# The recurrence's slot table: stages five slots apart, the new state formed ahead of the outputs, the solver, merges and compactions at other slots

## The chip, the cores and the metric

The kernel runs on one core of one Trainium2 chip. The metric is the time of one execution in microseconds (us) on the device. The core's engines work side by side, each through its own list of instructions in the order of the program: PE (TensorE, matrix products into PSUM), DVE (VectorE), ACT (ScalarE), POOL (GpSimd) and SP (SyncE, which here issues nearly all DMAs). An instruction that has to wait holds everything behind it on its engine.

## The reference, cut to what matters

For each of 32 pairs of batch and head a 40 by 40 state is carried through 768 steps, and each step gives an output row. The rows are then the tokens of two MLP layers in fp32.

```
for t in range(S):                      # S = 768, D = 40, B*H = 32
    y[:, :, t] = einsum('bhd,bhde->bhe', rt, state)
    Sa = einsum('bhde,bhe->bhd', state, at)
    state = state * wt[:, :, None, :] - einsum('bhd,bhe->bhde', Sa, bt) + einsum('bhd,bhe->bhde', vt, kt)
x = y.transpose(0, 2, 1, 3).reshape(3072, 320)
h = x @ w_in;  r = maximum(h, 0);  x = (r * r) @ w_out          # 320 -> 2048 -> 320
h = x @ w_in2; x = (h * cos(h)) @ w_out2
```

## The kernel before

**Chunks and periods.** The 768 steps are cut into 12 chunks of 64. `Program.period(c)` writes out the work around chunk `c`: 42 slots, and in each slot a few calls. `at(t, f)` puts a call into slot `t`; the calls of a slot run in the order in which `at` was called. There is no scheduler: the order in which the Python code calls the engines is the order on each engine, and semaphores are all that holds one engine against another. A slot has no time of its own.

**What a period does.** For chunk `c` there are four groups `g`, each a generator `state(c, g)` with six steps: `pq` (what the carried state gives), `px`, `pu`, `py` (each a set of small matmuls into PSUM and a copy or masked multiply out of it), and `pm`, which transposes the new state `MT` into `M0d` for the next chunk. Groups 0 and 1 run in the first half of a period, 2 and 3 in the second. Before the change `py` is followed, in one step, by four DVE operations a group: `MT += `, `sz += ` (outputs), `MT *= lam`, `yt = sz * lam` (outputs).

**The solver.** A chunk needs the inverse of a triangular matrix, for all 32 pairs. Its 32 by 32 diagonal blocks are inverted by `solve`, a chain of 31 pairs of instructions (`ttmp`, line 448, and `T`, line 451), each waiting for the one before, and a last copy (line 454). In period `c` it runs for chunk `c + 1`: on DVE in period 0 (as a chain fed in after other DVE instructions), on POOL from period 1 on, `rate[t]` instructions in slot `t`. `gt` and `gt_out` make and store the matrix (`Ls<-ga`, line 421; its last quarter is made in slots 0 to 2 of period `c` and stored in slot 3), `solve_load` (slot 6) loads it (`T<-kti`, `L<-Ls`, `l21<-Ls`), `solve_store` stores the result (`Tn<-L`, `Ts<-T`, lines 461 and 463), and `load_t` loads it in another layout (`t<-Tn`, `tt<-Ts`, lines 470 and 476). `merge` (matmuls `pw` and `pt`, copies of ACT at lines 491 and 504) makes the full inverse from it at the start of the next period.

**Other work in the slots.** `load_kb` (line 338, `cin<-cin`, 832 KB) loads k and b of chunk `c + 2`, `compact_kb` scales them on DVE (four instructions `cin<-cin` of 104 x 512), `compact_a` scales a (`at<-at`), `decay` makes `lam`. `mov_load` and `rv_load` bring v and r; `y_store` stores outputs (`xs<-yt`, line 547), and `load_x` (slot 2 of each second period) loads them as tokens (`xf<-xs`).

**The MLP in between.** From period 2 on, each slot also takes on average 64.2 / 42 = 1.53 pairs of matmuls of layer 0 (`h`, line 839, and `po`, line 795). A hidden tile goes through ACT (`g`, `gh`, lines 693 to 695) and POOL (`gl`, line 696). `h` has one PSUM buffer here, so PE cannot start a hidden tile before ACT has read the last one.

**The weights' pieces.** The MLP's weights come as 64-bit words that are taken apart on the chip, in every slot one step of `Weights`. For the second layer (`second`) a piece starts every five slots: its load (`w<-moe`, line 183, SP) in slot 5k of its own count, then in slot 5k + 4 `clamp` (ACT `u<-w`, line 167, and a DVE instruction), in 5k + 5 `bits` (DVE), in 5k + 6 `add` (POOL `u<-u,w`, line 179), and in 5k + 10 the store (`w2f<-u`, line 278, SP). The tiles `w` and `u` have two buffers each, so the clamp of a piece waits for its own load and for the store of the piece before the last, and these two stand side by side on SP. Counted in slots of the period, the pairs of load and store of the periods 4 to 10 stand at the slots that leave the rest 1, 4, 2, 0, 3, 1, 4 when divided by five. Before that, in period 2 and the start of period 3, `rest` has a piece every four slots, and `first` has one of 704 KB every five until about slot 30 of period 1.

The functions that the change touches, with the line numbers of the profile:

Of the kernel before, what the change touches and what calls it, by code (L numbers as in the profile page):

```python
# [15 lines left out]
ALU = mybir.AluOpType  # L16
# [265 lines left out]
class Attn:  # L282
# [269 lines left out]
    def state(self, c, g):  # L552
# [42 lines left out]
        last = c == self.nch - 1  # L595
        if not last:
            self.vec.tensor_tensor(mt[0:104], yv[0:104, :, 64:104], mt[0:104], op=ALU.add)
        if c:
            self.vec.tensor_tensor(sz[0:104], yv[0:104, :, 0:64], sz[0:104], op=ALU.add)
        if not last:  # L600
            self.vec.tensor_tensor(mt[0:104], mt[0:104],
                                   self.lam[(c + 1) % 3][:, 4 * g:4 * g + 4, 64:65].to_broadcast([104, 4, 40]), op=ALU.mult)
# [271 lines left out]

ALONE = 2
FIRST, RATE = 9, 64.2 / 42


class Program:
# [131 lines left out]
    def period(self, c):  # L1013
# [6 lines left out]
        def at(t, f, *args):  # L1020
            todo.setdefault(t, []).append((f, args))

        for half in range(2):
            for k in range(5):
                for q in range(2):
                    at(20 * half + 4 * k, step, st[2 * half + q])
        for h, t0 in enumerate((5, 5) if c == 0 else (2, 2) if more else (4, 12)):
            mg = A.merge(h)
            at(t0, step, mg)
            at(t0 + (4 if c and more else 2), step, mg)  # L1030
        at(2, A.rv_load, c, 2)
        at(6, A.rv_load, c, 3)
        at(6, A.mov_load, c, 2)
        at(8, A.pmat, c, 2)
        at(14, A.mov_load, c, 3)
        at(16, A.pmat, c, 3)
        at(17, A.y_store, c, 0)
        at(37, A.y_store, c, 1)
        if more:
            for t in (0, 1, 2):  # L1040
                at(t, step, self.gts[c + 1])
            at(2, A.gt_in, c + 1, 0, 0)
            at(4, A.gt_in, c + 1, 0, 1)
            at(3, A.gt_out, c + 1, 1, 0)
            at(3, A.gt_out, c + 1, 1, 1)
            at(8, A.gt_in, c + 1, 1, 0)
            at(10, A.gt_in, c + 1, 1, 1)
            at(6, A.solve_load, c + 1)
            for t in range(9, 36):
                rate[t] = 3 if t % 3 == 0 else 2  # L1050
            rate[36] = 100
            at(37, A.solve_store)
            at(38, A.load_t)
            at(23, A.rv_load, c + 1, 0)
            at(25, A.rv_load, c + 1, 1)
            at(26, A.mov_load, c + 1, 0)
            at(28, A.pmat, c + 1, 0)
            at(34, A.mov_load, c + 1, 1)
            at(38, A.pmat, c + 1, 1)
        if c + 2 < nch:  # L1060
            for t in (0, 2, 3, 4, 5, 6, 7, 9):
# [7 lines left out]
            at(28, A.compact_a, c + 2, 1)  # L1069
            self.gts.setdefault(c + 2, A.gt(c + 2))  # L1070
            for t in (24, 25, 26, 32, 33, 34, 36, 37, 38):
                at(t, step, self.gts[c + 2])
            at(37, A.gt_out, c + 2, 0, 0)
            at(39, A.gt_out, c + 2, 0, 1)
        if c + 3 < nch:
            self.dcs[c + 3] = A.decay(c + 3)
            at(30, A.load_w, c + 3)
            for t in (34, 35, 36, 38, 40, 41):
                at(t, step, self.dcs[c + 3])
        for t in range(42):  # L1080
            if more and t == 9:
# [116 lines left out]
```

## Time and profile before

| | |
|---|---|
| time, median of 3 runs | 1291.59 us (1290.32 to 1296.13) |
| the profiled execution | 1293.38 us, of which 1291.6 us are its span |
| PE busy | 1075.1 us, 83% |
| DVE, ACT, POOL busy | 712.9, 702.4, 671.1 us (55%, 54%, 52%) |
| granted TensorE clock, mean | 0.897 of full speed |
| chain that ended last, by engine | PE 50%, POOL 16%, DMA 12%, DVE 10%, SP's queue 5% |

How to read it: the span is cut by the program into a start without the MLP (to about 200 us), the periods with the MLP in between (to about 864 us), and the rest of the MLP alone (864 to 1291.6 us). In the last part PE is busy nearly all the time; in the periods it is not. The shares of the whole span say little: what a change in the periods is worth is read in a period.

### The profile page before, as it was taken

The page shows a single profiled execution, that of the slowest core. Times are in us where ns is not written, and L with a number is a line of the kernel's source. Part 1 is how long each engine was busy: PE and PEld are TensorE (multiplying, and loading weights), DVE is VectorE, ACT ScalarE, POOL GpSimd, SP SyncE. Part 2 cuts the span into 40 slices and gives each one's busy share as a digit, 9 for nine tenths or more (in the row PEclk, how much of TensorE's full clock was granted, in tenths as well). Part 3 has the DMA queues.
Part 4 walks back from the last instruction along what each step waited for, and adds up shares of the span by engine and source line. Part 5 has one row for each costly group of instructions (what it writes and reads, how often), then busy time and mean ns, then how long its engine had stood idle before and what let it go on. Part 6 is the DMA issues. An engine that isn't in the chain of part 4 may idle for free.

```text
span 1291.6 us, 27044 instructions
## 1 busy us (share of the span) xinstructions
PE 1075.1 (83%) x10242; PEld 902.2 (70%) x10242; DVE 712.9 (55%) x1450; ACT 702.4 (54%) x1492; POOL 671.1 (52%) x1067
## 2 busy tenths in 40 slices
PE   3245636787879898969797899799999999999997
PEld 3144536666657676757676678578889999999996
DVE  6869765576656665736665546221197343444432
ACT  4133644566566566655656556556556565655554
POOL 4112585685739482838474747423586333333332
PEclk9985555788979898988898889899999999999998
DMA  6473744546373838373745454413031010101000
GB/s 178 83 170 92 174 113 97 115 94 137 71 182 93 171 82 190 93 156 84 159 128 119 113 131 114 88 41 134 19 117 41 5 46 1 46 1 45 1 21 24
DMA packets 281168, 121.74 MB, mean 94 GB/s; under 512 B 231013, under 2 KB 259173, under 8 KB 279885
## 3 DMA queue, kind: packets, MB, share of 16 engines
q1 hardware_dynamic: 279195, 119.24, 38.8%
q8 instruction: 83, 1.36, 0.4%
q10 hardware_dynamic: 1834, 0.69, 0.2%
q14 instruction: 56, 0.46, 0.1%
HBM read 91.31 MB, written 28.57 MB: 93 GB/s over the span
## 4 chain that ended last, share of the span: by engine, by line
PE 50%; POOL 16%; DMA 12%; DVE 10%; SPq 5%; issue 4%; ACT 3%; POOLq 0%; ACTq 0%; DVEq 0%
PE h L839 22%; PE pt L785 13%; PE po L795 7%; DMA cin<-cin 6%; POOL T L451 5%; POOL ttmp L448 4%; POOL gl L696 3%; DMA w2f<-u 2%; POOL u L179 2%; PE px L573 2%; DVE u L142 2%; DVE T L451 1%; DVE ttmp L448 1%; DVE cin L142 1%; PE pu L581 1%
## 5 line engine op out<-in xcount | busy, mean ns | idle before, releaser
L839 PE MATMUL h<-xh,ws 128*128 128x512 f32 x960 | 333.8, 411 | 22.5 <-ACT g L693 22.2
L839 PE MATMUL h<-xl,ws 128*128 128x512 f32 x576 | 235.5, 409 | 0.0
L839 PEld LDWEIGHTS h<-xh,ws 128*128 128x128 f32 x960 | 185.9, 195 | 66.2 <-ACT g L693 26.2
L724 POOL TENSOR_TENSOR gl<-g,gh 128x512 fp32r<-128x512 f32 x96 | 125.2, 1304 | 190.9 <-ACT gh L723 163.6
L179 POOL TENSOR_TENSOR u<-u,w 128x256 int32<-128x256 int32 (+2 forms) x104 | 75.4, 725 | 222.0 <-DVE u L142 142.3
L696 POOL TENSOR_TENSOR gl<-g,gh 128x512 fp32r<-128x512 f32 x96 | 126.7, 1320 | 116.8 <-ACT gh L695 108.9
L142 DVE TENSOR_SCALAR u<-u 128x256 f32<-128x256 f32 (+2 forms) x208 | 72.5, 349 | 172.9 <-ACT u L167 171.2
L795 PE MATMUL po<-gh,ws 128*128 128x512 f32 x480 | 142.8, 422 | 0.3 <-DVE o L142 0.3
L448 POOL TENSOR_TENSOR ttmp<-T,L 128x126 f32<-128x126 f32 (+22 forms) x310 | 124.9, 403 | 34.0 <-DMA L<-Ls 14.0
L451 POOL TENSOR_TENSOR T<-T,ttmp 128x126 f32<-128x126 f32 (+22 forms) x310 | 131.3, 424 | 19.3
L785 PE MATMUL pt<-ws,gh 128*128 128x320 f32 x768 | 128.1, 308 | 0.5 <-DVE g L142 0.4
L839 PEld LDWEIGHTS h<-xl,ws 128*128 128x128 f32 x576 | 112.5, 195 | 20.2
L785 PEld LDWEIGHTS pt<-ws,gh 128*128 128x128 f32 x768 | 119.9, 188 | 8.3 <-DVE g L142 0.6
L142 DVE SCALAR_TENSOR_TENSOR g<-n,h 128x512 f32<-128x512 int32 x96 | 66.0, 687 | 103.3 <-ACT n L704 100.4
L704 ACT ACTIVATE n<-h 128x512 int32<-128x512 f32 x96 | 57.3, 596 | 119.9 <-PE h L839 119.8
L693 ACT ACTIVATE g<-h 128x512 f32<-128x512 f32 x96 | 57.0, 594 | 109.8 <-PE h L839 109.2
L407 PE MATMUL pgt<-at,cin 40*128 40x104 f32 x768 | 72.1, 329 | 52.1 <-DVE at L142 21.4
L795 PEld LDWEIGHTS po<-gh,ws 128*128 128x128 f32 x480 | 94.0, 201 | 24.0 <-issue 1.7
L142 DVE TENSOR_TENSOR g<-g,h 128x512 f32<-128x512 f32 x96 | 65.8, 685 | 71.7 <-ACT g L708 71.7
L167 ACT ACTIVATE u<-w 128x256 f32<-128x256 f32 (+2 forms) x104 | 40.8, 392 | 117.9 <-DMA w2f<-u 73.7
L407 PEld LDWEIGHTS pgt<-at,cin 40*128 40x128 f32 x768 | 62.0, 230 | 59.1 <-issue 24.9
L795 PE MATMUL po<-gl,ws 128*128 128x512 f32 x288 | 85.5, 400 | 0.0
(100 smaller groups left out, 2308.5 us busy)
## 6 DMA issues: line engine op xcount, KB each, us to landing
rv<-rv SPq DMA_DIRECT2D x48, 256.0 KB
cin<-cin SPq DMA_DIRECT2D x11, 832.0 KB
w<-moe SPq DMA_DIRECT2D x12, 704.0 KB
w<-moe SPq DMA_DIRECT2D x40, 160.0 KB
Ls<-ga SPq DMA_DIRECT2D x48, 128.0 KB
L<-Ls SPq DMA_DIRECT2D x48, 128.0 KB
wr<-w2f SPq DMA_DIRECT2D x16, 352.0 KB
w<-moe SPq DMA_DIRECT2D x20, 256.0 KB
```

Of the source, the lines that this page charges most:

```text
L142: fn(*args, **kwargs)
L179: self.nc.gpsimd.tensor_tensor(t.bitcast(I32), u.bitcast(I32), w[:, :, 0], op=ALU.add)
L407: nc.tensor.matmul(pv[par][:, j], self.kb[r0:r0 + 40, p0 + j].rearrange("p h b -> p (h b)"), self.at[r0:r0 + 40, p0 + j], start=True, stop ...
L448: eng.tensor_tensor(tv, T[:, 0:r, j:j + 1].to_broadcast([128, r, n]), L[:, j:j + 1, j + 1:32].to_broadcast([128, r, n]), op=ALU.mult)
L451: eng.tensor_tensor(T[:, 0:r, j + 1:32], T[:, 0:r, j + 1:32], tv, op=ALU.add)
L693: nc.scalar.activation(g, h, AF.Relu)
L696: self.later.append((2, lambda: nc.gpsimd.tensor_tensor(gl, g, gh, op=ALU.subtract)))
L704: nc.scalar.activation(n, h, AF.Copy, bias=0.25, scale=float(np.float32(1.0 / (2.0 * np.pi))))
L724: nc.gpsimd.tensor_tensor(gl, g, gh, op=ALU.subtract)
L785: nc.tensor.matmul(self.pos[j][:, 0:DM], x[:, 128 * j:128 * j + 128], wo[:, DM * ws:DM * ws + DM], start=(f == 0 and x is gh and ws == 0), ...
L795: nc.tensor.matmul(self.pos[m], wo[:, 128 * ws:128 * ws + 128], x, start=(f == 0 and k in (0, 2, 4)), stop=(f == NF - 1 and k in (5, 6, 7)))
L839: nc.tensor.matmul(h, wi[:, ws], x[:, kt], start=(k == 0), stop=(k == 7))
```

## The change

The diff changes numbers in the slot table and the order inside one step, and no instruction's form. In `state`, `MT *= lam` moves up behind `MT +=`, and a `yield` is put in: the two output operations become a step of their own, one (first half: slot 16) or two (second half: slot 37) slots later. The first five stages stand five slots apart instead of four, so `pm` stands at slot 20 instead of 16, and at 41 instead of 36. The merges stand at 3 and 7 in all periods. The solver still starts in slot 9, has three instructions in two of three slots (before: in one of three), and ends in slot 32 (before: 35), with what is left in slot 33 (before 36). `solve_store` moves from slot 37 to 34, `load_t` from 38 to 36, `compact_kb` from 10, 12, 14, 16 to 13, 15, 17, 19.

```
-            for k in range(5):
+            for k in (0, 5, 10, 15, 16, 20):
                 for q in range(2):
-                    at(20 * half + 4 * k, step, st[2 * half + q])
-        for h, t0 in enumerate((5, 5) if c == 0 else (2, 2) if more else (4, 12)):
+                    at(21 * half + k - (half and k < 16), step, st[2 * half + q])
+        for h in range(2):
             mg = A.merge(h)
-            at(t0, step, mg)
-            at(t0 + (4 if c and more else 2), step, mg)
+            at(3, step, mg)
+            at(7, step, mg)
-        at(6, A.mov_load, c, 2)
-        at(8, A.pmat, c, 2)
-        at(14, A.mov_load, c, 3)
-        at(16, A.pmat, c, 3)
-        at(17, A.y_store, c, 0)
-        at(37, A.y_store, c, 1)
+        at(7, A.mov_load, c, 2)
+        at(10, A.pmat, c, 2)
+        at(16, A.mov_load, c, 3)
+        at(18, A.pmat, c, 3)
+        at(19, A.y_store, c, 0)
+        at(40, A.y_store, c, 1)
-            for t in range(9, 36):
-                rate[t] = 3 if t % 3 == 0 else 2
-            rate[36] = 100
-            at(37, A.solve_store)
-            at(38, A.load_t)
+            for t in range(9, END):                   # END = 33
+                rate[t] = 2 if t % 3 == 0 else 3
+            rate[END] = 100
+            at(END + 1, A.solve_store)
+            at(END + 3, A.load_t)
-            at(34, A.mov_load, c + 1, 1)
+            at(37, A.mov_load, c + 1, 1)
-            for t in (10, 12, 14, 16):
+            for t in (13, 15, 17, 19):
                 at(t, step, ck)
-            at(37, A.gt_out, c + 2, 0, 0)
-            at(39, A.gt_out, c + 2, 0, 1)
+            at(34, A.gt_out, c + 2, 0, 0)
+            at(36, A.gt_out, c + 2, 0, 1)
```

Three places of the program show what moves; all are of period 6.

SP, from the load of `w` ahead of `solve_store` to the loads of the next solver, before:

```order
253 L183 DMA w<-moe 128x320
254 L278 DMA w2f<-u 128x256
255 L518 DMA mov<-vt 64x4x40 x2
256 L547 DMA xs<-yt 40x8x64 x2
257 L461 DMA Tn<-L 64x512
258 L463 DMA Ts<-T 1024x1x32 x2
259 L421 DMA Ls<-ga 64x8x64
260 L183 DMA w<-moe 128x320
261 L278 DMA w2f<-u 128x128
262 L470 DMA t_120<-Tn 32x32x16 x2
263 L476 DMA tt<-Ts 32x16x32 x4
264 L421 DMA Ls<-ga 64x8x64
```

and after, the same stretch:

```order
253 L183 DMA w<-moe 128x320
254 L278 DMA w2f<-u 128x256
255 L461 DMA Tn<-L 64x512
256 L463 DMA Ts<-T 1024x1x32 x2
257 L421 DMA Ls<-ga 64x8x64
258 L470 DMA t_120<-Tn 32x32x16 x2
259 L476 DMA tt<-Ts 32x16x32 x4
260 L421 DMA Ls<-ga 64x8x64
261 L518 DMA mov<-vt 64x4x40 x2
262 L183 DMA w<-moe 128x320
263 L278 DMA w2f<-u 128x128
264 L547 DMA xs<-yt 40x8x64 x2
```

The store of the solver's result and the loads that read it back now stand ahead of `mov<-vt`, of `xs<-yt` and of the pair `w<-moe`, `w2f<-u`, which stood between store and loads.

POOL, the end of the solver, before:

```order
567 L448 TENSOR_TENSOR ttmp<-T,L 128x45
568 L451 TENSOR_TENSOR T<-T,ttmp 128x15x3
569 L448 TENSOR_TENSOR ttmp<-T,L 128x30
570 L179 TENSOR_TENSOR u<-u,w 128x128
571 L696 TENSOR_TENSOR gl<-g,gh 128x512
572 L451 TENSOR_TENSOR T<-T,ttmp 128x15x2
573 L448 TENSOR_TENSOR ttmp<-T,L 128x16
574 L451 TENSOR_TENSOR T<-T,ttmp 128x16
575 L454 COPY L<-T 64x512
```

and after:

```order
567 L448 TENSOR_TENSOR ttmp<-T,L 128x45
568 L451 TENSOR_TENSOR T<-T,ttmp 128x15x3
569 L448 TENSOR_TENSOR ttmp<-T,L 128x30
570 L451 TENSOR_TENSOR T<-T,ttmp 128x15x2
571 L448 TENSOR_TENSOR ttmp<-T,L 128x16
572 L451 TENSOR_TENSOR T<-T,ttmp 128x16
573 L454 COPY L<-T 64x512
574 L179 TENSOR_TENSOR u<-u,w 128x128
575 L696 TENSOR_TENSOR gl<-g,gh 128x512
```

The last `u` and `gl` that stood inside the solver stand behind it: five of each before, four of each now in this period.

DVE around the first compaction (`cin<-cin 104x512`) and `MT` of the first half, before:

```order
654 L142 TENSOR_TENSOR cin<-cin 104x512
655 L142 TENSOR_SCALAR u<-u 128x128
656 L142 TENSOR_TENSOR MT_111<-py,MT_111 104x160
657 L142 TENSOR_TENSOR sz<-py,sz 104x256
658 L142 TENSOR_TENSOR MT_111<-MT_111,lam_94 104x160
659 L142 TENSOR_TENSOR yt<-sz,lam_93 104x256
...
665 L142 TENSOR_SCALAR u<-u 128x128
666 L142 SCALAR_TENSOR_TENSOR u<-w,u 128x128
```

and after:

```order
660 L142 TENSOR_SCALAR u<-u 128x128
661 L142 SCALAR_TENSOR_TENSOR u<-w,u 128x128
662 L142 TENSOR_TENSOR cin<-cin 104x512
663 L142 TENSOR_TENSOR MT_111<-py,MT_111 104x160
664 L142 TENSOR_TENSOR MT_111<-MT_111,lam_94 104x160
665 L142 TENSOR_TENSOR MT_112<-py,MT_112 104x160
666 L142 TENSOR_TENSOR MT_112<-MT_112,lam_94 104x160
```

The two instructions of a piece's `bits` stand ahead of the compaction now, ten instructions behind it before, and both groups' `MT` are complete ahead of any output operation.

## Rows read from the trace of the kernel before

**Rows 1.** Windows, solver to solver: length, busy of PE, PEld, DVE, ACT, POOL, clock, DMA

```profile
507.30:574.30 67.00, 57.31 (x710) 45.38 (x710) 39.28 (x90) 41.24 (x96) 41.51 (x81) 0.92 0.56 127
sum 547.00, PE 466.20 PEld 370.21 DVE 330.76 ACT 322.93 POOL 347.87; mean PE 58.28 PEld 46.28 DVE 41.35 ACT 40.37 POOL 43.48
```

**Rows 2.** Timeline of POOL, first and last solver instructions: start, length, engine, operation, [idle before]

```profile
507.25 0.25 POOL L448 TENSOR_TENSOR ttmp<-T,L 128x31 f32<-128x31 f32 x1
...
516.33 0.79 POOL L179 TENSOR_TENSOR u<-u,w 128x128 int32<-128x128 int32 x1 [4.70 <-ACT o L746]
517.08 1.29 POOL L696 TENSOR_TENSOR gl<-g,gh 128x512 fp32r<-128x512 f32 x1
...
551.16 1.03 POOL L454 COPY L<-T 64x512 f32<-64x512 f32 x1
```

**Rows 3.** Timeline of SP between the solvers of periods 6 and 7

```profile
552.22 0.49 SPq L461 DMA_DIRECT2D Tn<-L  x1
552.75 1.38 SPq L463 DMA_DIRECT2D Ts<-T  x2
...
555.57 0.43 SPq L278 DMA_DIRECT2D w2f<-u  x1
556.09 0.98 SPq L470 DMA_DIRECT2D t<-Tn  x2
557.17 2.33 SPq L476 DMA_DIRECT2D tt<-Ts  x4
...
561.93 1.26 SPq L421 DMA_DIRECT2D Ls<-ga  x2
...
564.94 1.98 SPq L518 DMA_DIRECT2D mov<-vt  x2
```

**Rows 4.** Timelines of ACT and PE at the end of period 6

```profile
557.78 0.34 ACT L167 ACTIVATE u<-w 128x160 f32<-128x160 f32 x1 [10.37 <-DMA w2f<-u]
...
559.47 1.92 PE L487 MATMUL pw<-t,l 32*32 32x32 f32 x64 [8.56 <-ACT sz L568]
```

**Rows 5.** Waits of DVE and PE: who for whom, us in total, times, longest

```profile
DVE cin L142 <- DMA cin<-cin: 58.1, 12, 7.6
PE pm L614 <- DVE MT L142: 36.3, 16, 10.7
```

**Rows 6.** Timelines of PE: first matmul of slot 20, and of slot 0 after period 6

```profile
518.70 0.25 PE L563 MATMUL pq<-rv,M0d 40*40 40x64 f32 x1
...
547.11 0.25 PE L563 MATMUL pq<-rv,M0d 40*40 40x64 f32 x1
```

**Rows 7.** Timelines of SP and ACT in period 4: another store and the clamp it held

```profile
355.87 0.43 SPq L278 DMA_DIRECT2D w2f<-u  x1
...
360.37 0.34 ACT L167 ACTIVATE u<-w 128x160 f32<-128x160 f32 x1 [9.24 <-DMA w2f<-u]
```

**Rows 8.** Timelines of POOL and DVE in period 4: a solver instruction beside `at<-at`, and alone

```profile
390.27 0.94 POOL L448 TENSOR_TENSOR ttmp<-T,L 128x126 f32<-128x126 f32 x1
...
392.82 0.42 POOL L451 TENSOR_TENSOR T<-T,ttmp 128x126 f32<-128x126 f32 x1
...
390.26 0.68 DVE L142 TENSOR_TENSOR at<-at,lam 104x512 f32<-104x512 f32 x1
```

**Rows 9.** Timelines of DVE and PE: periods 0, and 11 behind the last solver's store

```profile
94.61 0.69 DVE L142 TENSOR_TENSOR cin<-cin 104x512 f32<-104x512 f32 x1 [5.18 <-DMA cin<-cin]
...
816.68 0.50 PE L839 MATMUL h<-xh,ws 128*128 128x512 f32 x1 [2.29 <-ACT g L693]
```

**Rows 10.** Timelines of SP: result stored, and last store of the next matrix, periods 2 and 9

```profile
280.56 0.49 SPq L461 DMA_DIRECT2D Tn<-L  x1
...
290.03 1.26 SPq L421 DMA_DIRECT2D Ls<-ga  x2
...
755.98 0.48 SPq L461 DMA_DIRECT2D Tn<-L  x1
...
768.15 1.31 SPq L421 DMA_DIRECT2D Ls<-ga  x2
```

More of the change, by code (lines that the diff above doesn't have):

```diff
@@ L597, in state @@
             self.vec.tensor_tensor(mt[0:104], yv[0:104, :, 64:104], mt[0:104], op=ALU.add)
+            self.vec.tensor_tensor(mt[0:104], mt[0:104],
+                                   self.lam[(c + 1) % 3][:, 4 * g:4 * g + 4, 64:65].to_broadcast([104, 4, 40]), op=ALU.mult)
+        yield
         if c:
             self.vec.tensor_tensor(sz[0:104], yv[0:104, :, 0:64], sz[0:104], op=ALU.add)
-        if not last:
-            self.vec.tensor_tensor(mt[0:104], mt[0:104],
-                                   self.lam[(c + 1) % 3][:, 4 * g:4 * g + 4, 64:65].to_broadcast([104, 4, 40]), op=ALU.mult)
         if g % 2 == 0:
@@ L873, in step @@
             break
-ALONE = 2
+END = 33
 FIRST, RATE = 9, 64.2 / 42
@@ L1048, in period @@
             at(6, A.solve_load, c + 1)
-            for t in range(9, 36):
-                rate[t] = 3 if t % 3 == 0 else 2
-            rate[36] = 100
-            at(37, A.solve_store)
-            at(38, A.load_t)
+            for t in range(9, END):
[3 more added lines that the diff above has]
+            at(END + 3, A.load_t)
             at(23, A.rv_load, c + 1, 0)
             at(25, A.rv_load, c + 1, 1)
-            at(26, A.mov_load, c + 1, 0)
-            at(28, A.pmat, c + 1, 0)
-            at(34, A.mov_load, c + 1, 1)
-            at(38, A.pmat, c + 1, 1)
+            at(22, A.mov_load, c + 1, 0)
+            at(25, A.pmat, c + 1, 0)
+            at(37, A.mov_load, c + 1, 1)
+            at(39, A.pmat, c + 1, 1)
         if c + 2 < nch:
-            for t in (0, 2, 3, 4, 5, 6, 7, 9):
+            for t in (1, 3, 4, 6, 8, 9, 11, 12):
                 at(t, step, self.dcs[c + 2])
@@ L1065, in period @@
             ck = A.compact_kb(c + 2)
[L1066 removed]
+            for t in (13, 15, 17, 19):
                 at(t, step, ck)
             at(20, A.compact_a, c + 2, 0)
[L1069 removed]
+            at(29, A.compact_a, c + 2, 1)
             self.gts.setdefault(c + 2, A.gt(c + 2))
[L1071 removed]
+            for t in (23, 24, 25, 30, 31, 32, 35, 36, 37):
                 at(t, step, self.gts[c + 2])
[L1073 to L1074 removed]
+            at(34, A.gt_out, c + 2, 0, 0)
+            at(36, A.gt_out, c + 2, 0, 1)
         if c + 3 < nch:
@@ L1077, in period @@
             at(30, A.load_w, c + 3)
-            for t in (34, 35, 36, 38, 40, 41):
+            for t in (37, 38, 39, 40, 41, 41):
                 at(t, step, self.dcs[c + 3])
```

## The prediction

> **What bounds the kernel now.** I read the page first. Its slices show a last third in which PE is busy nearly all the time, and periods before it in which it is not; the change is in the periods. So I cut those by windows, from the first instruction of one solver to that of the next. Eight of them, periods 2 to 9, are 547.0 us, 68.4 us each, with PE busy 58.3 and POOL 43.5 [rows 1]. No engine is full, so a chain must close from period to period. The timelines of POOL and SP in period 6 (67.0 us, near the mean) show it. The reader is to see two stretches.
>
> *First, the solver on POOL*: from 507.25 to the end of its copy at 551.16 + 1.03 = 552.19, 44.9 us [rows 2]. Its 62 dependent instructions share POOL with `u` and `gl` of the MLP, and POOL stood 4.7 us in front of one `u` [rows 2]. The row names ACT as the releaser, but the DVE work that makes this `u` stands behind the first compaction, which waits for `load_kb`: DVE spent 58.1 us in 12 such waits [rows 5]. So a DMA that DVE waits for stops the solver.
>
> *Second, from the solver's end to the next solver's start*, 574.3 - 552.2 = 22.1 us. SP waits at `Tn<-L` for POOL and then issues without a pause: result stored, read back, pieces, and at 561.93 the last store of the next matrix, `Ls<-ga` [rows 3]. That is 9.7 us behind the solver; over the eight periods the same distance is 11.3 us on the mean, from 9.5 in period 2 to 12.2 in period 9 [rows 10]. From this store to the next solver it takes 574.3 - 561.9 = 12.4 us.
>
> While SP waits, the pieces' stores wait behind it. ACT stood 10.37 us for such a store, and PE then 8.56 us for ACT [rows 4]. Not only DMAs are late then: every engine is.
>
> **The change part by part.**
>
> *Spacing and MT.* A slot takes (547.11 - 518.70) / 22 = 1.29 us where nothing is held [rows 6]. `pm` waited 36.3 us for MT in 16 places [rows 5]. Now MT is done before the outputs and has five slots, some 6.5 us, instead of four. I take this wait as gone. But PE has 68.4 - 58.3 = 10 us of room a period, so this alone ends nothing sooner: PE would reach the next wait earlier. I cost it at nothing; what hides it is the chain of POOL and SP, and if that were gone, the 36.3 us would be the gain.
>
> *Solver denser, 24 slots for 27.* POOL lags behind its slots, so no rate makes it faster. What helps is that less stands inside: one `gl` and about half a `u` less. That is 1.29 + 0.79 / 2 = 1.7 us [rows 2].
>
> *Compactions three slots later.* In period 6 the `bits` of the first piece come ahead of the compaction now, and the 4.7 us should vanish. In other periods the piece falls on the other side: pieces stand every five slots, periods shift by two. `load_kb` also goes out later, since `mov<-vt` (1.98 us) is now issued ahead of it instead of ahead of the solver's loads [rows 3]. So the gain lies between 0 and 4.7 us. I take 2.2, near the middle, because about half of the phases are like period 6. Solver: 44.9 - 1.7 - 2.2 = 41.0.
>
> *`solve_store` from slot 37 to 34.* This adds a wait. SP now stops three slots earlier for a solver that ends only some 4 us earlier, and behind it stand `load_t`, `mov<-vt`, the pieces and `xs<-yt`. In period 6 the pair of slot 37 now follows `load_t` and `mov`. Counted from the solver's end with the durations of [rows 3]: Tn 0.5, Ts 1.4, Ls 0.7 with gaps, t and tt 3.5, Ls 0.7, mov 1.3, pair 1.0, together 9.1 us. Before, its store was issued at 555.57, 3.4 us behind the end. The store then takes 2.2 us (555.57 to 557.78, [rows 3, 4]) to 4.5 us (355.87 to 360.37, [rows 7]); I take 3.0 behind the issue. So ACT goes on about 12 us behind the solver's end, at slot 41, and needs 561.93 - 557.78 = 4.1 us to the store of the matrix [rows 3, 4]: 16.2 us instead of 9.7.
>
> The same count by phase: pairs of slots 36 (periods 4, 9) hold ACT at slot 40 and give 16.5; slot 38 (periods 3, 8) 14.7; slots 34 and 39, or 35 and 40 (periods 5, 7) 15.3 and 14.2, since there the first store goes out right behind Ts; period 2, with its pieces every four slots, 16. Mean 15.5, against 11.3: plus 4.2 us. The bounds are 0 (the clamps are not late enough to matter) and 6.5 (every period like the sixth).
>
> *`mov<-vt` out of the way of the solver's loads*: minus 1.0 us of the 12.4, half of the 1.98 us of its row being a wait that something else will show [rows 3].
>
> *The merge one slot later* no longer waits for the result; that PE wait was not on the chain either.
>
> Sum for a period: -1.7 - 2.2 + 4.2 - 1.0 = -0.7, with rounding -0.8; eight times, -6.4 us.
>
> *Period 0 and 1.* In period 0 the solver is on DVE, and DVE stood 5.18 us for `load_kb` [rows 9]. Now four slots with ten solver instructions stand ahead of the compaction instead of one slot with three, and I take most of that wait as filled: -4.4. Before the solvers of periods 1 and 2, `mov` is gone from the loads: -1.3 each. Together -7. Period 1 has no piece behind slot 30, so nothing is held there.
>
> *Periods 10 and 11.* The last solver is not followed by another; what counts is PE. ACT is held at slot 38, about 11 us long, until 6 us behind the solver's end. Before, three waits of PE around the same point, the first of 2.29 us [rows 9], made 6.2 us. So +5.
>
> Sum: -6.4 - 7 + 5 = -8.4 us. From the profiled execution, 1293.4, this gives 1285.0. That execution stands 1.8 us above the median, 1291.59, so I say **1283 us**.
>
> *A price that only a page gives.* The rows put the landing of a `w2f<-u` at 2.2 and at 4.5 us. The Trainium skill, "DMA: Bandwidth & Descriptors", section on the anatomy of one DMA, fits 2.0 us plus the bytes at 436 KB per us, for DMAs issued by GpSimd; 80 KB would land in an estimated 2.2 us. By it ACT would go on 0.8 us sooner in each of eight periods, and the sum would be 1277. The second row is twice that, so I keep 3.0.
>
> *A rule against this change.* A solver instruction that took 0.42 us alone took 0.94 beside `at<-at` of DVE [rows 8]. The Trainium skill, "SBUF: State Buffer", section "Who interferes with whom", says that a DVE instruction with two SBUF inputs and a GpSimd instruction that reads SBUF lock each other out. The trace agrees with it. All four compactions are now inside the solver, while before the first ran in POOL's pause; by rule and row that is 0.5 us a period, and the sum would be 1287.
>
> **The rivals.**
>
> *The overlap works.* The pieces' holds matter little and the stall at `load_kb` vanishes everywhere: solver 44.9 - 1.7 - 3.7 = 39.5, matrix stored 12.8 behind it (11.3 and the `mov` and `xs<-yt` that now come in between), then 11: 63.3 us, 5 less a period, -41 in eight, -7 at the start, 0 at the end: 1244. With holds in half of the periods about 1260. For it speaks that PE would have room (58.3 busy of 63.3); against it the 10.37 us of [rows 4], where the hold is seen.
>
> *Slower: SP stops too early.* The mechanism is the wait at slot 34 alone. If the compaction still stops the solver (it waits for the same `load_kb`, which now goes out later), the solver takes 43.2, the store of the matrix comes 16.5 behind it and the rest 11: 70.7, 2.3 more than 68.4 a period, +18; start -5, end +9: 1313. It decides as soon as the hold costs more than about 5.5 us a period.
>
> *It doesn't do what it says.* The solver is not done by slot 33 because POOL is the limit, and what the slots move is given back at the next wait: 1291, give or take 5.
>
> **How the numbers follow.** Forecast (1275 to 1290): 0.33. Overlap (1240 to 1270): 0.25. Slower (1300 to 1320): 0.25. Nothing (1286 to 1296): 0.17. About 0.5% is what a measurement of this kernel can tell from no change, 6.5 us, so faster means below 1285.1 and slower above 1298. Of the forecast, 0.22 is faster and 0.11 the same; of "nothing", 0.12 is the same and 0.05 slower, the slower rival is slower. Faster 0.47, same 0.23, slower 0.30. The range leaves out the better end of the overlap and the worse end of the slower case, a tenth each: 1256 to 1309.
>
> **What would show it.** In the new profile: the solver, first `ttmp` to its copy, at 41 us instead of 45, without a `u` that waits 4 us; `pm` waiting for MT no more; ACT waiting for `w2f<-u` 7 to 12 us in each period, with the end of that wait about 11 us behind `Tn<-L`; the last `Ls<-ga` some 15 us behind `Tn<-L`. If that distance is still 11, the overlap is right; if the solver is still at 44, the slower rival. It would be wrong altogether if the periods were no longer closed by POOL and SP, and PE became full.

## The result, and the profile after

The changed kernel takes **1301.31 us** (median of 7 runs, 1297.15 to 1304.29) against 1293.01 us of the kernel before on the same chip: ratio 1.0056, 95% interval 1.0035 to 1.0077. It is slower by half a per cent. The forecast was 1283 us; the time lies in its range, on the other side of no change.

The profiled execution has a span of 1299.4 us, 7.8 more than before. From the first solver of period 2 to that of period 10 it was [rows 1] and is now, with the one cycle of period 6 (windows: length, busy of PE, PEld, DVE, ACT, POOL, clock, DMA; the second line is the eight periods taken as one window):

```profile
509.50:579.60 70.10, 58.92 (x719) 46.10 (x712) 43.01 (x88) 40.09 (x94) 42.27 (x80) 0.93 0.56 130
...
sum 555.10, PE 478.58 PEld 376.27 DVE 347.51 ACT 322.43 POOL 350.27; mean PE 478.58 PEld 376.27 DVE 347.51 ACT 322.43 POOL 350.27
```

The eight periods grew from 547.0 to 555.1 us, 8.1 in all. The granted clock over them was 0.89 before and is 0.90 now, so it is not what made them longer. The solver itself became faster. The rows that answer to [rows 2], from the timeline of POOL:

```profile
509.48 0.24 POOL L448 TENSOR_TENSOR ttmp<-T,L 128x31 f32<-128x31 f32 x1
...
516.92 0.80 POOL L179 TENSOR_TENSOR u<-u,w 128x128 int32<-128x128 int32 x1 [2.26 <-DVE u L142]
517.72 1.29 POOL L696 TENSOR_TENSOR gl<-g,gh 128x512 fp32r<-128x512 f32 x1
...
549.87 1.34 POOL L454 COPY L<-T 64x512 f32<-64x512 f32 x1
```

The stall of 4.70 us is 2.26, and the copy ends 41.7 us behind the first instruction (44.9 before). So the time went into the stretch behind the solver. The timeline of SP from the end of this solver, which answers to [rows 3] (start, length of all issues of the row, DMA, number):

```profile
551.24 0.48 SPq L461 DMA_DIRECT2D Tn<-L  x1
551.75 1.38 SPq L463 DMA_DIRECT2D Ts<-T  x2
553.23 0.62 SPq L421 DMA_DIRECT2D Ls<-ga  x1
553.95 1.24 SPq L470 DMA_DIRECT2D t<-Tn  x2
555.35 3.14 SPq L476 DMA_DIRECT2D tt<-Ts  x4
558.53 0.60 SPq L421 DMA_DIRECT2D Ls<-ga  x1
559.24 1.24 SPq L518 DMA_DIRECT2D mov<-vt  x2
560.58 0.54 SPq L183 DMA_DIRECT2D w<-moe  x1
561.16 0.43 SPq L278 DMA_DIRECT2D w2f<-u  x1
561.69 0.82 SPq L547 DMA_DIRECT2D xs<-yt  x2
562.61 0.36 SPq L183 DMA_DIRECT2D w<-moe  x1
563.02 0.64 SPq L278 DMA_DIRECT2D w2f<-u  x1
563.76 0.37 SPq L510 DMA_DIRECT2D rv<-rv  x1
565.24 1.77 SPq L421 DMA_DIRECT2D Ls<-ga  x2
567.11 0.57 SPq L183 DMA_DIRECT2D w<-moe  x1
567.73 0.43 SPq L278 DMA_DIRECT2D w2f<-u  x1
568.26 0.38 SPq L510 DMA_DIRECT2D rv<-rv  x1
568.69 0.42 SPq L434 DMA_DIRECT2D T<-kti  x1
569.22 4.34 SPq L437 DMA_DIRECT2D L<-Ls  x4
573.65 1.13 SPq L439 DMA_DIRECT2D l<-Ls  x2
```

The reader is to see that this list has few holes. SP does little here but issue: 30 DMAs stand between the end of the solver and `l<-Ls`, the last loads that the next solver's chunk needs, and most of them take SP 0.3 to 0.7 us each, 22.4 us in all. The holes are at the last stores, `Ls<-ga`, where SP waited 1.0 and 0.5 us for DVE's `ga`. The table sets the parts of the cycle side by side. It is counted from such timelines of SP and POOL in periods 2 to 9 (means, us); "last store" is the start of the row of the last two `Ls<-ga`, as in the prediction.

| | before | after |
|---|---|---|
| solver, first instruction to end of copy | 45.1 | 41.4 |
| end of copy to last store of the matrix (`Ls<-ga`) | 11.4 | 14.9 |
| from there to the first `l<-Ls` | 8.6 | 7.7 |
| from there to the next solver's first instruction | 3.3 | 5.3 |
| DMA issues of SP between copy and `l<-Ls` | 28.0 | 31.1 |

From the copy to `l<-Ls` the way grew by 2.7 us. The issues and the usual pauses between them (under 0.2 us) make 1.2 of that; the other 1.5 are longer holes, 2.2 us a period instead of 0.7, in which SP waited for DVE at `Ls<-ga` or, at `L<-Ls`, for the last `Ls` to land.

The waits that answer to [rows 5] and [rows 4] (who for whom, us in total, times, longest):

```profile
DVE cin L142 <- DMA cin<-cin: 18.1, 5, 6.5
...
PE pm L614 <- DVE MT L142: 18.7, 4, 8.9
...
ACT u L167 <- DMA w2f<-u: 87.2, 24, 10.6
```

The waits at which the change aimed are smaller: 58.1 us became 18.1 for the compactions, 36.3 became 18.7 for MT. Of PE's four remaining waits for MT, three lie in periods 0 and 1 (16.8 of the 18.7 us). ACT's holds at the pieces' stores grew, from 73.7 us in 20 places to 87.2 in 24, but not where the prediction had them: those that end in the 16 us behind the solvers of periods 2 to 9 made 39.7 us before and make 37.7 now. What grew lies inside the solvers (27.7 to 38.8 us) and behind the last one.

### The profile page after: what moved, and what is told of

It reads as the page before. It is cut to its first block, busy times and chain, and to the rows that moved or that the text cites. A ratio compares the mean times of both kernels' runs of the same rounds, so it can differ in the third digit from the quotient of the medians.

```text
span 1299.4 us, 27060 instructions
## 1 busy us (share of the span) xinstructions
PE 1080.7 (83%) x10242; PEld 902.3 (69%) x10242; DVE 736.1 (57%) x1450; ACT 700.8 (54%) x1492; POOL 675.8 (52%) x1067
## 4 chain that ended last, share of the span: by engine, by line
PE 53%; DVE 13%; POOL 11%; DMA 9%; ACT 5%; issue 4%; SPq 4%; ACTq 0%; POOLq 0%; DVEq 0%
PE h L839 23%; PE pt L785 13%; PE po L795 7%; POOL T L451 3%; DMA w2f<-u 3%; POOL ttmp L448 3%; DMA cin<-cin 3%; PE pgt L407 2%; PE px L573 2%; DVE cin L142 2%; DVE mov L142 2%; DVE u L142 2%; POOL gl L696 1%; POOL u L179 1%; DVE T L451 1%
## 5 line engine op out<-in xcount | busy, mean ns | idle before, releaser
L839 PE MATMUL h<-xh,ws 128*128 128x512 f32 x960 | 331.9, 410 | 23.3 <-ACT g L693 21.7
L407 PE MATMUL pgt<-at,cin 40*128 40x104 f32 x768 | 78.4, 341 | 74.1 <-DVE at L142 27.7
L407 PEld LDWEIGHTS pgt<-at,cin 40*128 40x128 f32 x768 | 67.1, 239 | 85.4 <-issue 24.0
L167 ACT ACTIVATE u<-w 128x256 f32<-128x256 f32 (+2 forms) x104 | 40.9, 393 | 136.2 <-DMA w2f<-u 87.2
L795 PE MATMUL po<-gl,ws 128*128 128x512 f32 x288 | 91.7, 412 | 0.0
```

The costliest lines, as they stand in the source:

```text
L407: nc.tensor.matmul(pv[par][:, j], self.kb[r0:r0 + 40, p0 + j].rearrange("p h b -> p (h b)"), self.at[r0:r0 + 40, p0 + j], start=True, stop ...
L795: nc.tensor.matmul(self.pos[m], wo[:, 128 * ws:128 * ws + 128], x, start=(f == 0 and k in (0, 2, 4)), stop=(f == NF - 1 and k in (5, 6, 7)))
L839: nc.tensor.matmul(h, wi[:, ws], x[:, kt], start=(k == 0), stop=(k == 7))
```

## The experiments

The prediction's own reason is called **theory H**: SP's stop at slot 34 (its wait at `Tn<-L` for the end of the solver) holds the pieces' stores, these hold ACT, ACT holds the front (the front is the slot at which PE, ACT, DVE and POOL stand; all that these engines feed to SP is as late as it is). Its first rival, **P**: the five-slot spacing and the later merges make the front late by themselves. Ratios are to the kernel before, with 95% intervals; 1% is 12.9 us.

**e1: store late, all else as changed.**

```diff
-            at(END + 1, A.solve_store)
-            at(END + 3, A.load_t)
+            at(37, A.solve_store)
+            at(38, A.load_t)
```

> The changed kernel (1301.3 us) with the solver's result stored from slot 37 and read back from slot 38, as in the kernel before; all else as changed. Theory H (SP stops at slot 34 and holds the pieces, so ACT, so the front, so the next solver): the distance from the solver's copy to the last store of the matrix goes from 14.9 back to about 12 us, that from this store to the next solver from 13.0 to about 12, the solver stays at 41.4; 3 to 4 us less in each of eight periods, 1266 to 1280 us. Rival P (the five-slot spacing, the later merges and compactions make the front late by themselves): the distances stay at 15 and 13, 1297 to 1305 us. Rival R (a later store is a later matrix): the first distance grows, 1305 us or more.

Measured: 1276.2 us, 0.9847 (0.9819 to 0.9874). The early store alone costs 27 us (1.0056 less 0.9847). Copy to last store 13.2 us, `l<-Ls` to next solver 4.3, solver 41.4. The time is that of H; the first distance fell only by 1.7. The rival R of the expectation, that a later store makes a later matrix, is out.

**e2: the pieces' DMAs from ACT's queue, store early as changed.**

```diff
-        self.nc.sync.dma_start(w, self.i[nm][f].bitcast(I32).rearrange("p (a b) -> p a b", b=2)[:, c0:c0 + n])
+        eng = self.nc.scalar if nm == "moe2" else self.nc.sync
+        eng.dma_start(w, self.i[nm][f].bitcast(I32).rearrange("p (a b) -> p a b", b=2)[:, c0:c0 + n])
...
-        return self.pieces("moe2", range(NF), 5, lambda f, c0, u: self.nc.sync.dma_start(
+        return self.pieces("moe2", range(NF), 5, lambda f, c0, u: self.nc.scalar.dma_start(
```

> The changed kernel with the second layer's pieces (load w<-moe and store w2f<-u) issued by ACT instead of SP; the early store of the solver's result stays. It takes the hold away and leaves SP's stop. Theory H: ACT's waits for w2f<-u (73 us in periods 2 to 9) mostly vanish, copy to matrix store 10 to 12 us, 1255 to 1280 us. Rival P: the waits vanish but the distances stay, 1297 to 1305 us. A third way: the issues take ACT's own time, some 17 a period, and ACT becomes late by itself: 1300 us or more with ACT's idle time gone.

Measured: 1293.3 us, 0.9985 (0.9968 to 1.0001). The holds are gone:

```profile
ACT u L167 <- DMA w2f<-u: 12.8, 8, 4.5
```

and yet copy to last store is still 14.6 us. Only 9 us of the 27 came back. Taken strictly H fails here as the whole reason; but SP now paused more between its issues (7.0 us from the copy to `l<-Ls`, 4.2 in the changed kernel), so this run does not settle it.

**e3: the kernel before with the compactions moved, nothing else.**

```diff
-            for t in (10, 12, 14, 16):
+            for t in (13, 15, 17, 19):
                 at(t, step, ck)
```

> The kernel before (1293.0 us) with the compactions of kb at slots 13, 15, 17, 19 instead of 10, 12, 14, 16, and nothing else. The prediction's term: DVE's wait for cin falls from 58 to about 20 us and the solver from 45.1 to about 43, 2.2 us in eight periods and 4 in period 0: 1270 to 1278 us if the rest of the period stands. Rival: what the solver gains is waited for elsewhere (SP or the front), 1290 to 1296 us. Rival by the lock of DVE and GpSimd: solver at 45 or more, 1296 to 1300 us.

Measured: **1269.1 us, 0.9806** (0.9781 to 0.9830). The solver took 43.1 us, DVE's wait for `cin` 12.4 us in all, and the first solver of period 2 began at 222.6 instead of 233.7. One line of the change is worth 25 us. All four compactions ran inside the solver here, and it became 2.0 us faster. POOL's waits in front of a `u` or `gl` inside the solver fell from 3.8 to 1.4 us a period. The prediction weighed a rule of the Trainium skill against this, "SBUF — State Buffer", section "Who interferes with whom": a DVE instruction with two SBUF inputs and a GpSimd instruction that reads SBUF lock each other out. The row agreed with it (0.94 us beside `at<-at`, [rows 8]), but over a period it takes little: the solver's own 62 instructions were busy 25.6 us before and 25.9 in e3.

**e4: the kernel before with the spacing, MT first and the merges at 3 and 7, and the moves that the spacing forces** (the `mov` of the next chunk's second group from slot 34 to 37, since its buffer is now read until slot 35, and the output stores from 17 and 37 to 19 and 40). The decay of a later chunk is written over the one that the second half's outputs are scaled with, so those outputs differ; the order of all other work is the one meant.

```diff
-            for k in range(5):
+            for k in (0, 5, 10, 15, 16, 20):
...
-            at(34, A.mov_load, c + 1, 1)
-            at(38, A.pmat, c + 1, 1)
+            at(37, A.mov_load, c + 1, 1)
+            at(39, A.pmat, c + 1, 1)
```

> The kernel before with the stages five slots apart, MT formed ahead of the outputs, both merges at slots 3 and 7, and what has to go with them (mov of the next chunk's second group at slots 37 and 39, the output stores at 19 and 40); solver, compactions, stores and the rest as before. The prediction's term: PE's wait for MT (36.3 us) falls to about 10, and the time stays: 1289 to 1297 us. Theory P: the later merges and stages make the front late, 1298 to 1306 us. If PE's waits were on the chain: 1260 to 1280 us.

Measured: 1318.8 us, 1.0188 (1.0159 to 1.0217), worse than any theory gave. Copy to last store 13.8 us, although the store was at slot 37. I then counted the issues of SP behind the solver: 32.0 instead of 28.0, for `mov<-vt` and `xs<-yt` had slipped behind the solver's end. That gave **theory S**: behind the solver SP issues one DMA after the other, and the next matrix is loaded when all that stands ahead is issued.

**e5: e3 and these two moves, without the spacing.**

```diff
-            at(34, A.mov_load, c + 1, 1)
-            at(38, A.pmat, c + 1, 1)
+            at(37, A.mov_load, c + 1, 1)
+            at(39, A.pmat, c + 1, 1)
-        at(17, A.y_store, c, 0)
-        at(37, A.y_store, c, 1)
+        at(19, A.y_store, c, 0)
+        at(40, A.y_store, c, 1)
```

> The kernel of e3 (before, with the compactions moved: 1269 us, solver 43.1, from the solver's copy to the last load of the next matrix 20.0 us with 28 DMA issues of SP in between) with three lines of the change more: mov of the next chunk's second group at slot 37 instead of 34 (its products at 39), the output stores at 19 and 40 instead of 17 and 37. Stages, merges and solver stay as before. Theory S (behind the solver SP issues one DMA after the other, some 0.7 us each, and the next matrix is loaded when all that stands ahead is issued): 32 issues, 2.5 us more in each of eight periods and a little at the start, 1286 to 1294 us. Theory H (the hold of ACT) and theory P (the stages' spacing): 1267 to 1273 us.

Measured: 1294.2 us, 0.9992 (0.9979 to 1.0006): 24 us above e3 for four DMA issues, at the upper end of what S said. Timelines of SP behind the solver of period 6, e3 and then e5:

```profile
536.10 0.49 SPq L461 DMA_DIRECT2D Tn<-L  x1
...
543.43 0.61 SPq L421 DMA_DIRECT2D Ls<-ga  x1
...
555.20 2.11 SPq L439 DMA_DIRECT2D l<-Ls  x2
```

```profile
549.01 0.48 SPq L461 DMA_DIRECT2D Tn<-L  x1
...
551.16 1.25 SPq L518 DMA_DIRECT2D mov<-vt  x2
...
558.52 1.06 SPq L547 DMA_DIRECT2D xs<-yt  x2
...
570.73 2.46 SPq L439 DMA_DIRECT2D l<-Ls  x2
```

From `Tn<-L` to `l<-Ls` it is 19.1 us in e3 and 21.7 in e5. The two rows that came in between take 1.25 and 1.06 us and a gap of 0.1 each. e5 costs over e3 what e4 costs over the kernel before (1.86% and 1.88%), so the spacing with MT and merges costs nothing by itself that could be told from zero (the intervals leave some 5 us); P falls.

**e6: e3 with three issues fewer ahead of the matrix.**

```diff
-        at(6, A.rv_load, c, 3)
-        at(6, A.mov_load, c, 2)
-        at(8, A.pmat, c, 2)
+        at(7, A.rv_load, c, 3)
+        at(7, A.mov_load, c, 2)
+        at(10, A.pmat, c, 2)
```

> The kernel of e3 with the load of rv for the fourth group and of mov for the third at slot 7, behind the loads of the solver (before: slot 6, ahead of them), and its products at slot 10: three DMA issues fewer between the solver's end and the next matrix. Theory S: 25 issues, 17.9 us instead of 20.0, 2 us less in each of eight periods, 1250 to 1258 us. Theories H and P: 1267 to 1273 us.

Measured: 1274.2 us, 0.9854 (0.9829 to 0.9880), 6 us above e3 and no gain: a miss. 25.0 issues, and `l<-Ls` 18.6 us behind the copy instead of 20.0; but the next solver then began 4.3 us behind it instead of 3.2, and took 44.2 us instead of 43.1. Loading sooner gains nothing as soon as POOL is not there yet: the solver stands in POOL's queue behind the `gl` and `u` of the slots before. Two chains end almost together, SP's issues and the front. Why the solver itself became longer is not shown. The changed kernel moves one of these two loads too, `mov` from slot 6 to 7.

**e7: e3 with MT ahead of the outputs, four slots apart.**

```diff
-            for k in range(5):
+            for k in (0, 4, 8, 12, 13, 16):
...
+            self.vec.tensor_tensor(mt[0:104], mt[0:104],
+                                   self.lam[(c + 1) % 3][:, 4 * g:4 * g + 4, 64:65].to_broadcast([104, 4, 40]), op=ALU.mult)
+        yield
```

> The kernel of e3 with the new state formed ahead of the outputs (MT at slot 12, outputs at slot 13 of each half), the stages four slots apart as before. Theory S and the prediction's term (PE is not on the chain, the wait for MT costs nothing): 1265 to 1272 us, PE's wait for MT gone. If PE's waits are on the chain: 1240 to 1262 us.

Measured: 1274.5 us, 0.9839 (0.9810 to 0.9868), the interval overlaps that of e3. PE's wait for MT fell from 7.3 us in e3 to 3.2 in all, and it bought nothing.

**e8 and e9: the solver's rate of the change, store at slot 37,** on e6 and on e3.

```diff
-            for t in range(9, 36):
-                rate[t] = 3 if t % 3 == 0 else 2
-            rate[36] = 100
+            for t in range(9, 33):
+                rate[t] = 2 if t % 3 == 0 else 3
+            rate[33] = 100
```

> The kernel of e6 with the changed kernel's rate of the solver (done by slot 33), its result still stored from slot 37. Theory S: the solver falls from 43.1 to 41.4 us as in the changed kernel, the stretch behind it stays at 18: 12 to 16 us below e6, 1236 to 1246 us. If the solver's rate in the order does nothing (POOL lags anyway): as e6.

> The kernel of e3 (compactions moved) with the solver's rate of the change (done by slot 33), its result stored from slot 37 as before; rv and mov loads where they were (unlike e8). Theory S: 28 issues again, but e6 showed that three fewer bring nothing because the solver's start then waits for the front: within 6 us of e8, 1253 to 1265 us, solver 41.4. If the three issues do count: 1266 to 1275 us.

Measured: e8 1259.1 us, 0.9732 (0.9705 to 0.9758), 15 us below e6 as expected, and above the absolute range only because e6 had missed; e9 1256.4 us, 0.9698 (0.9678 to 0.9719). The solver takes 41.4 and 40.4 us. The rate is worth 14 us (0.9806 less 0.9698), and e6's three issues are again worth nothing (e8 is not below e9). The solver gained more than that, 2.7 us a period from e3 to e9, but the store in slot 37 now comes 1.2 us behind its end.

**e10 and e11: e9 with the store at slot 34 (read back at 36), and at 36 (37).**

> The kernel of e9 with the solver's result stored from slot 34 and read back from slot 36, as in the change; the stages stay four slots apart. Theory S: mov (2 issues), the output stores (2) and about one issue of the pieces come behind the solver's end, 33 issues instead of 28, about 3 us more behind the solver, less the 1.2 us by which the store of slot 37 came late: 12 to 22 us above e9, 1268 to 1285 us. If the early store cost only together with the five-slot spacing: as e9, within 6 us.

> The kernel of e9 with the store from slot 36 and the reading back from slot 37. Theory S: the output stores (2 issues) and half an issue of the pieces more behind the solver's end, 1.5 us, against the 1.2 us by which the store at slot 37 comes late in half of the periods: within 6 us of e9.

Measured: e10 **1286.6 us, 0.9936** (0.9924 to 0.9948), 31 us above e9 and above what I expected; e11 1265.9 us, 0.9777 (0.9762 to 0.9793), 10 us above e9, a miss by 4 us. Three slots earlier cost all that compactions and rate had brought, but for 8 us. Issues from the end of the solver to `l<-Ls`, counted by time: 29.4, 33.1 and 30.6 in e9, e10 and e11 (in e9 some go out before the late store).

**e12: e9 with the first half of the next matrix stored from slots 34 and 36** (formed a slot or two earlier), as in the change.

```diff
-            for t in (24, 25, 26, 32, 33, 34, 36, 37, 38):
+            for t in (23, 24, 25, 30, 31, 32, 35, 36, 37):
                 at(t, step, self.gts[c + 2])
-            at(37, A.gt_out, c + 2, 0, 0)
-            at(39, A.gt_out, c + 2, 0, 1)
+            at(34, A.gt_out, c + 2, 0, 0)
+            at(36, A.gt_out, c + 2, 0, 1)
```

> The kernel of e9 with the first half of the next matrix formed one to two slots earlier and stored from slots 34 and 36 instead of 37 and 39, as in the change: two issues fewer behind the solver. Theory S alone: 26 issues, 1.3 us less a period, about 10 us below e9. With the front as the next limit, as in e6: 0 to 5 us below e9.

Measured: **1251.2 us, 0.9656** (0.9642 to 0.9669), the fastest of all: 3.4% below the kernel before, 4.0% below the changed one. It is 5 us below e9, half of what S alone gave and the end of what was expected with the front as the next limit.

**e13: e10 with `mov` and the output stores at slot 33, ahead of the stop; e14: e12 with these two there as well, the matrix stored from 33 and 35, the result from 36.**

```diff
-            at(34, A.mov_load, c + 1, 1)
+            at(33, A.mov_load, c + 1, 1)
-        at(37, A.y_store, c, 1)
+        at(33, A.y_store, c, 1)
```

> The kernel of e10 (store of the solver's result from slot 34, 1286.6 us) with the mov load of slot 34 and the output stores of slot 37 both at slot 33, ahead of SP's stop; the pieces stay behind it as in e10, so ACT is held for their stores as before. Theory S (the issues behind the solver count): 29 issues instead of 33, some 2.5 us less a period, 1260 to 1270 us. Theory H (the pieces' hold of ACT counts): 1282 to 1290 us.

> The kernel of e12 (1251.2 us) with the same two moved ahead to slot 33, the first half of the next matrix stored from slots 33 and 35, and the solver's result stored from slot 36 and read back from 37. Theory S: nothing more comes behind the solver than in e12, and the 1.4 us by which the store of slot 37 comes late vanish: 1238 to 1247 us. If the front is the limit by now: 1248 to 1254 us.

Measured: e13 1269.4 us, 0.9791 (0.9765 to 0.9818), 29.1 issues; four issues taken back are worth 19 us (11.8 of them in periods 2 to 9: 533.3 us instead of 545.1), while ACT's holds did not shrink. The row of ACT's waits in e10, then in e13:

```profile
ACT u L167 <- DMA w2f<-u: 106.8, 30, 9.9
```

```profile
ACT u L167 <- DMA w2f<-u: 116.7, 29, 10.4
```

e14 1254.8 us, 0.9684 (0.9664 to 0.9704): no gain over e12. One issue fewer than in e12 (26.9 and 27.9 by time), and the solver again starts later behind its loads (3.8 us instead of 3.3). That agrees with the second of the two answers expected, that the front is the limit there.

**e15, e16, e17: e9, e10 and e12 with the pieces standing still in slots 34 to 41.**

```diff
             if c >= 2:
-                step(self.w2, 1)
+                step(self.w2, t < 34)
```

> The kernel of e9 (1256.4 us) in which the pieces' generator stands still in slots 34 to 41 of each period, so that no piece is loaded, clamped or stored there (they end a period later). Both theories: fewer issues behind the solver and no hold of ACT there, 1235 to 1250 us; if the front is held by something else, 1250 to 1257 us.

> The kernel of e10 (store of the solver's result from slot 34, 1286.6 us) with the same standstill in slots 34 to 41: nothing of the pieces stands behind SP's stop, only mov, the output stores and the matrix. Theory S: four issues more behind the solver than in e15, 12 to 22 us above e15. Theory H (the early store costs by the pieces' hold alone): 0 to 5 us above e15.

> The kernel of e12 (1251.2 us) with the same standstill in slots 34 to 41. Theory S: two issues fewer than in e15, 0 to 8 us below e15.

Measured: e15 1270.3 us, 0.9825 (0.9807 to 0.9842); e16 1291.9, 0.9984 (0.9970 to 0.9998); e17 1265.4, 0.9791 (0.9771 to 0.9810). e15 misses on the absolute side; e16 and e17 stand to it as expected, 21 us above and 4 below. The reason for the miss shows in the windows from the first solver of period 10 to the last matmul of the attention, and from there to the end, e9 and then e15:

```profile
743.70:826.40 82.70, 76.04 (x855) 58.98 (x851) 29.85 (x72) 45.88 (x107) 44.92 (x85) 0.94 0.31 74
826.40:1254.70 428.30, 419.01 (x2242) 372.61 (x2242) 179.53 (x267) 238.50 (x398) 183.87 (x163) 0.99 0.12 40
```

```profile
737.80:812.60 74.80, 71.99 (x871) 56.76 (x867) 32.75 (x78) 47.55 (x113) 44.98 (x87) 1.00 0.36 90
812.60:1268.50 455.90, 421.23 (x2242) 374.41 (x2242) 190.98 (x300) 244.15 (x418) 190.09 (x175) 0.96 0.14 44
...
845.36 0.19 PE L932 MATMUL pb<-kc,worst 104*1 104x1 f32 x2 [25.34 <-DVE worst L142]
```

The attention ended 13.8 us sooner than in e9, as both theories had it. Behind it the same 2242 instructions of PE took 27.6 us longer, because PE stood 25.34 us for DVE: the pieces that had stood still are taken apart there, ahead of `worst` on DVE. e16 and e17 have the same wait of 25.3 us, so it drops out between the three. The difference is what counts: e16 is 20.6 us above e15 with four issues more (30.0 and 26.0), and the holds behind the stop are gone in both. ACT's row is 73.6 us in 22 places in e15 and 67.1 in 25 in e16, but none of these waits ends in the 20 us behind a solver, save one of 0.2 us in e16 (e9 has 24.4 us there, e10 51.6). So S holds for 20 of the 31 us that the early store costs in e10. In periods 2 to 9 alone it is 13.9 us (530.3 less 516.4) of 25.8 (545.1 less 519.3), about half.

## Why the prediction was wrong

By its own steps, from the spans of the two profiled executions, the first three rows for a period and the rest in all (us; the prediction's three terms add up to -0.7, and it went on with -0.8):

| step | predicted | measured |
|---|---|---|
| solver | -3.9 | -3.7 |
| copy to last store | +4.2 | +3.6 |
| last store to next solver | -1.0 | +1.1 |
| eight periods | -6.4 | +8.1 |
| periods 0 and 1 | -7 | -1.4 |
| periods 10 and 11 | +5 | +3.5 |
| behind the attention | 0 | -2.4 |
| sum | -8.4 | +7.8 |

**The solver was right, and for the reasons given.** The compactions were put at 2.2 us a period and 4.4 in period 0, 22 us; e3 measured 25, though with 11.1 at the start. The rate was put at 1.7 us a period, 13.6 in all; e8 and e9 measured 14 and 15, here with some luck, since the solver gained 2.7 and the late store took a part back. One `gl` and 0.75 of a `u` less a period stand inside the solver, nearly what the prediction counted. MT and spacing were put at nothing, and e7 and the pair e4, e5 show nothing that can be told from it. The 2.4 us behind the attention come with the spacing: there e1, e2, e4 and the changed kernel take 426 us, the kernels without it 428 (those of e15 to e17, which wait there for the pieces, aside).

**Copy to last store had the right size and mostly the wrong reason.** I counted SP's issues behind the solver, but only up to the pieces' store that releases ACT, and let ACT's hold carry the cost from there. e10 against e13 and e16 against e15 show that the issues themselves are the larger part of the whole and about half of it inside periods 2 to 9. Of the 31 us of the early store in e10, 20 remain without a hold behind the stop; the other third, some 10 us, comes and goes with the pieces. The 9 us that e2 won by taking the holds away fit this, though fewer issues of SP are in them too. The holds themselves tell why the prediction gave them too much: it took period 6 as its pattern, where the hold ended 5.6 us behind the solver before and 12.1 after, just as it said. In the other periods from 3 to 9 it had ended 10.2 to 11.4 us behind the solver already. Of the signs that the prediction named, the solver at 41 us and the last store at 15 came true; the hold of 7 to 12 us was there in three periods of eight.

**Last store to next solver is the step that failed.** Its first part behaved: last store to `l<-Ls` fell by 0.9 us, nearly the 1.0 predicted for `mov<-vt` (the rest became a wait of SP for `Ls` to land). The row of the whole run, before and after:

```profile
SPq L437 <- DMA Ls<-ga: 1.5, 2, 0.9
...
SPq L437 <- DMA Ls<-ga: 10.8, 11, 2.9
```

Its second part was not in the prediction at all: I put the distance from `l<-Ls` to the solver at no change, as if the solver started when its loads land. The POOL timeline in period 9 of the changed kernel shows what happened instead; the last `l<-Ls` had been issued by 779.2:

```profile
776.47 0.46 POOL L179 TENSOR_TENSOR u<-u,w 128x128 int32<-128x128 int32 x1 [9.26 <-DVE u L142]
780.52 1.26 POOL L696 TENSOR_TENSOR gl<-g,gh 128x512 fp32r<-128x512 f32 x1 [3.59 <-ACT gh L695]
786.14 1.27 POOL L696 TENSOR_TENSOR gl<-g,gh 128x512 fp32r<-128x512 f32 x1 [4.36 <-ACT gh L695]
787.38 0.24 POOL L448 TENSOR_TENSOR ttmp<-T,L 128x31 f32<-128x31 f32 x1
```

POOL waits twice for ACT, and the solver begins without a wait of its own right behind the second `gl`. ACT had lost its time in two waits:

```profile
764.71 0.43 ACT L167 ACTIVATE u<-w 128x256 f32<-128x256 f32 x1 [7.89 <-DMA w2f<-u]
...
773.43 1.63 ACT L491 ACTIVATE l<-pw 32x256 f32<-32x256 f32 x4 [4.20 <-PE pw L487]
```

The first is the hold; with the late store of e1 such holds behind the solver make 19.0 us in periods 2 to 9, with the early one 37.7. That it alone made the `gl` late is not shown here, since the wait for the merge's `pw` stands between. In the kernel before, in the same place, the solver did wait for its loads:

```profile
777.67 1.29 POOL L696 TENSOR_TENSOR gl<-g,gh 128x512 fp32r<-128x512 f32 x1 [2.11 <-ACT gh L695]
780.66 0.24 POOL L448 TENSOR_TENSOR ttmp<-T,L 128x31 f32<-128x31 f32 x1 [1.70 <-DMA L<-Ls]
```

Of the eight starts that the table counts, four waited for `L<-Ls` before, 3.7 us in all, and one after, 0.2 us; after the change seven of the eight stand right behind a `gl` that had waited 0.8 to 5.0 us for ACT. The mean from `l<-Ls` to the solver was 3.3 us before and 5.3 after, and the runs give both halves of this. One microsecond is the gain at `mov<-vt` given back: where loads are taken from ahead of the matrix and nothing else is done (e6 against e3), `l<-Ls` comes sooner and the distance grows from 3.2 to 4.3, and e1, which has `mov` out of the way too, also shows 4.3. The other is the hold: the early store adds 1.0 (e1 to the changed kernel) or 1.3 (e9 to e10), and only 0.1 where no hold stands behind the stop (3.5 in e15, 3.7 in e16); e2, with the early store and the holds gone, shows 4.0. The prediction had named this hold, but put it into the distance to the last store alone and left it out of POOL's queue. The step is wrong by 2.1 us, eight times, 17 us, and that is nearly the whole distance between -8.4 and +7.8.

**The start failed for the same wrong reason.** For period 1 the prediction said that nothing is held there because no piece stands behind slot 30. For S pieces don't matter. e3 brings the first solver of period 2 forward by 11.1 us, more than the 4.4 given to the compactions there; the four issues of e5 push it back by 7.0 without any piece of the second layer there, and the changed kernel keeps 1.4.

The parts add up. In us: compactions -25.1 (e3), rate -14.0 (e9 less e3), first half of the matrix earlier -5.4 (e12 less e9), `mov` and output stores behind the solver +24.1 (e5 less e3), early store +27.0 (changed kernel less e1): together +6.6, where +7.2 was measured. That it fits so closely is in part luck, since the intervals leave the sum some 6 us either way. It also leaves out what no run tested alone: `mov` of slot 6 at 7 (in e6 with `rv`, there 6 us slower), and three moves that the printed diff leaves out, the decay, the first `mov` from slot 26 to 22 and the second half of `compact_a` from 28 to 29. Three good edits are worth 44 us, and the other two cost 51. The rival "slower: SP stops too early" had the sign and the place, but not the way: it needed compactions that still stop the solver, and these no longer do.

## What to carry to other kernels

- Between the end of one serial step and the start of the next, count the DMA issues on the queue that serves both, and do not look at the bytes alone. If the queue has no holes there, each issue put behind the step costs about its own duration in every cycle, whatever it is for; put it ahead of the point where the queue waits.
- A wait that is moved to an earlier place in a queue keeps its end and takes along all that stood between the two places. The same four DMAs issued ahead of the wait gave back 19 us (e13 against e10).
- When two chains end within a microsecond or two of each other, adding to one shows at once and taking away from it shows nothing (e5 against e6); ask of each first instruction which of its inputs came last.

## What the runs showed that I had not expected

- Four DMA issues, of 0.5 to 0.6 us each, cost 24 us of 1270 (e5). In periods 2 to 9 that is 2.4 us a period (549.7 us less 530.5); the two rows of e5 with their gaps make 2.5.
- Issuing the pieces from ACT's queue took most of ACT's holds away (87.2 us became 12.8) and made SP wait instead: `L<-Ls`, the matrix's own load, waited 10.6 us in three places for a `w<-moe` that another engine had issued. The trace of e2 shows what couples the two queues: the program's DMAs report on eight semaphores, whichever engine issues them, and in all three places `L<-Ls` waits for the one that it shares with that `w<-moe`, until this has landed. No run gave the pieces semaphores of their own.
- The best order found is e12, which is the kernel before with three edits of the change (compactions, the solver's rate, the matrix's first half) and without the other two: 1251.2 us.
